# A 2:4-sparse matmul on one core: a new order for the first transposes and their copies, with five tiles of x loaded one by one

## The chip, the cores and the metric

The kernel runs on one core of a Trainium2 chip. The metric is the device time of one execution in microseconds (us), as the median of several runs. Beside it there is one execution recorded by the profiler, whose trace gives every instruction's start and duration; times inside the kernel are given from the start of that trace's span.

## The reference

```python
B, S, D = 16, 512, 1024
def reference(x, w, b):                    # x [16, 512, 1024], w [1024, 1024], b [1024], bf16
    wg = w.reshape(D // 4, 4, D)           # groups of four rows that follow each other
    mag = jnp.abs(wg)
    order = jnp.argsort(mag, 1)
    thr = jnp.take_along_axis(mag, order[:, 2:3, :], 1)    # second largest of the four
    wp = (wg * (mag >= thr)).reshape(D, D)
    return jnp.einsum("bsd,df->bsf", x, wp) + b
```

Of every four neighbouring rows of w only the two largest in each column survive. The pruned matrix is multiplied by 8192 rows of x, and a bias is added.

## The kernel before, in words

**Tiles.** x has 64 tiles of 128 rows. The contraction of 1024 is eight blocks of 128; the halves of it are called groups g = 0 and 1. A block of g = 0 or 1 comes in two layouts. In the "packed" layout (`w_sb`, `wp`) a partition holds one group of four rows, so the four members m = 0..3 of the group lie side by side and pruning is elementwise. In the "natural" layout (`wp_nat`) the rows lie in their own order, one row per partition; DMAs called `spread` (L139) make it from `wp`.

**The head.** While weights arrive and are pruned, TensorE has only what is ready. Tiles 0 to 7 (called NPK) are multiplied with the packed weights of g = 0, as soon as each piece of `wp` exists. Each needs x with the contraction on the partitions, so TensorE transposes the tile in four steps of 128x128 against an identity (`transpose`, L184; four matmuls at L189 into one PSUM buffer `tp`), and ScalarE copies the result to SBUF (`copy_xt`, L192, the copy at L194). The pool `psum_t` (L58) has two buffers, so a transpose waits for the copy of the transpose two before it. `mm_piece` (L205, matmuls at L216) multiplies a transposed tile with one piece of `wp`; a piece is 256 columns of g = 0. Two tiles share one PSUM bank of the pool `psum_o` (L59, six banks), by the list `pairs` (L201): (5, 6), (0, 1), (2, 3), (4, 7). When both tiles of a pair are done with a piece, ScalarE copies the bank to a staging tile (`stage`, L252, the copy at L256), and the bank comes free.

**Who sets the order.** The order on each engine in this head is written out by hand in `order` (L258), as a string of tokens per engine, and kept by program-order dependencies. On TensorE, `T7a` is the transpose of tile 7, `M7.0u` the matmul of tile 7 with piece 0, member 0 (u, v, s, t are members 0 to 3; x and y are pairs of members), `A0h0` the first half of a natural-layout output, `F8` eight dummy matmuls that keep the engine busy before data arrives. On ScalarE, `C7a` is the copy of tile 7's transpose and `S0b0` the staging copy of pair 0 (tiles 5 and 6), piece 0. On VectorE, `abs`, `hi`, `lo`, `t1`, `t2`, `thr`, `mask` and `mult` are the pruning steps; `mult0u` writes member 0 of piece 0 of `wp`. For the change these parts of the strings count:

```python
"pe":  "F8 T7a T5a T6a M7.0u M5.0u M7.0v M5.0v T1a M6.0u M6.0v T0a M7.0s M5.0s M6.0s M7.0t M5.0t M6.0t
        M1.0u M1.0v M1.0s M1.0t M0.0u M0.0v T4a M0.0s M0.0t T3a T2a M4.0u ... M2.0t M4.1x M5.1x M0.1x ..."
"act": "C7a C5a C6a C1a C0a C4a S0b0 C3a C2a S3b0 S1b0 S2b0 abs3 S3b1 ..."
```

**The first loads** are issued by two engines' queues, SyncE's (SP) and ScalarE's (ACT), in the order of L110 to L124. `load_w(g, c0, c1, ma, mb)` loads columns c0 to c1 of members ma to mb of the packed weights, `load_x(ta, tb)` the g = 0 half of tiles ta to tb-1 in one DMA. SP issues, in this order: member 0 and member 2 of weight piece 0 (64 KB each), tiles 5 and 6 in one DMA (256 KB), weight piece 1 (256 KB; "the second weights"), tile 4 (128 KB), tiles 2 and 3 (256 KB), pieces 2 and 3 (512 KB), half of g = 1 (512 KB), the bias, the other half of g = 1. ACT issues members 1 and 3 of piece 0, tile 7 (128 KB) and tiles 0 and 1 in one DMA (256 KB); then comes an activation on a dummy element (`spark`, L116) that brings in the activation table.

**Semaphores of the DMAs.** The framework gives the DMAs eight semaphores in turn. The ninth DMA, and each one after it, is issued only when the DMA eight before it has landed.

**The body and the tail.** After the head, tiles 8 to 63 go through natural-layout matmuls (`nat`, L239): x comes transposed by DMA, two banks per tile, VectorE adds the bias and writes bf16 (L400, L402), ScalarE's queue stores each tile in one DMA of 256 KB. The last `LATE` = 5 tiles are stored in halves (L457), the last tile in four parts.

Of the kernel before, what the change touches and what calls it, by code (L numbers as in the profile page):

```python
# [10 lines left out]
def kernel(  # L11
# [28 lines left out]
    NPK = 8  # L40
    LEAD = 4
    GROUPS = ((0, 5), (5, 8))
    LATE = 5
    sizes = (4, 8, 8, 8, 8, 8, 8)
    batches = []
    t0 = NPK + LEAD
# [29 lines left out]
    def act(i):  # L76
        return seq("act", i)
# [13 lines left out]
    def tokens(dram, t):  # L91
        a, b_ = next(s for s in GROUPS if s[0] <= t < s[1])
        return dram[a * P:b_ * P].rearrange("(p t) k -> p t k", p=P), t - a
    bias_sb = const.tile([P, Dout], bf16)

    def issue(eng, out_, in_):
        q = nc.sync if eng == "sp" else nc.scalar
        return seq(eng, q.dma_start(out_, in_))  # L98

    def load_w(g, c0, c1, ma=0, mb=4, eng="sp"):  # L100
        issue(eng, w_sb[:, g, ma:mb, c0:c1], wv[:, g, ma:mb, c0:c1])

    def load_x(ta, tb, eng="sp"):
        xs = const.tile([P, tb - ta, HK], bf16, name=f"x_{ta}")
        xv, n = tokens(xf, ta)
        issue(eng, xs[:], xv[:, n:n + tb - ta, :HK])
        for t in range(ta, tb):
            x_sb[t] = xs[:, t - ta, :]
# [3 lines left out]
    load_w(0, 0, 256, 2, 3)  # L112
    load_w(0, 0, 256, 3, 4, "act")
    load_x(7, 8, "act")
    load_x(0, 2, "act")
    act(nc.scalar.activation(spark[:], nc.const_aps.tensor(1.0, [P, 1], bf16), Act.Abs))  # L116
    load_x(5, 7)
    load_w(0, 256, 512)
    load_x(4, 5)
    load_x(2, 4)  # L120
    load_w(0, 512, 1024)
# [130 lines left out]
    def stage(q, n):  # L252
        if (q, n // 2) not in staged:
# [3 lines left out]

    order = {  # L258
        "pe": (
            "F8 T7a T5a T6a M7.0u M5.0u M7.0v M5.0v T1a M6.0u M6.0v T0a M7.0s M5.0s M6.0s M7.0t M5.0t M6.0t "  # L260
            "M1.0u M1.0v M1.0s M1.0t M0.0u M0.0v T4a M0.0s M0.0t T3a T2a M4.0u M4.0v M4.0s M4.0t "
            "M3.0u M3.0v M3.0s M3.0t M2.0u M2.0v M2.0s M2.0t M4.1x M5.1x M0.1x M7.1y M6.1y M2.1y M1.1y "
            "M3.1y M6.1x M4.1y M1.1x M3.1x M0.1y M7.1x M2.1x M5.1y M0.2 M3.2 M7.2 M1.2 M2.2 M4.2 "
            "M6.2 M0.3 M2.3 M5.3 M4.3 M5.2 M6.3 M3.3 M1.3 A0h0 A2h0 M7.3 A2h1 A1h0 A3h1 A0h1 A3h0 "
# [6 lines left out]
            "thr5 mask5 mult5"  # L271
        ),
        "act": (
            "C7a C5a C6a C1a C0a C4a S0b0 C3a C2a S3b0 S1b0 S2b0 abs3 S3b1 S1b1 S0b1 S2b1 S2b2 S1b2 "
            "S3b2 S0b2 S1b3 S2b3 W1.0q S3b3 S0b3"
        ),
        "sp": (
# [120 lines left out]
    def evac(o, ps, c0, c1, add=None):  # L398
        if add is None:
            dve(nc.vector.tensor_tensor(o[:, c0:c1], ps, bias_sb[:, c0:c1], op=Alu.add))  # L400
        else:
            dve(nc.vector.tensor_tensor(o[:, c0:c1].rearrange("p (n c) -> p n c", n=2),  # L402
                                        ps.rearrange("p (n c) -> p n c", n=2), add, op=Alu.add))
# [7 lines left out]
    def store(eng, t, o, c0=0, c1=Dout):  # L411
        issue(eng, rows(t)[:, c0:c1], o[:, c0:c1])
# [24 lines left out]
    for bi, (tb, nb) in enumerate(batches):  # L437
        if bi:
            load_batch(bi + 1)
        for j in range(nb):  # L440
# [9 lines left out]
            else:  # L450
# [4 lines left out]
                for h in range(2):  # L455
                    evac(o, pss[h][:], h * FH, (h + 1) * FH)
                    if t >= NT - LATE:  # L457
                        store("act", t, o, h * FH, (h + 1) * FH)
                if t < NT - LATE:
                    store("act", t, o)  # L460
# [30 lines left out]
```

## Time and profile before

| | |
|---|---|
| median of 3 runs | 233.41 us (233.27 to 234.06) |
| the profiled execution's own time | 233.83 us |
| span of its trace, first to last instruction | 232.0 us |
| TensorE (PE) busy | 228.0 us, 98% of the span, 1158 matmuls |
| VectorE (DVE) busy | 107.9 us, 46% |
| ScalarE (ACT) busy | 13.4 us, 6% |
| granted TensorE clock | full speed in all 40 slices |
| last store landed (store issue at 229.75 us, 1.5 us to landing) | 231.2 us |

The span leaves out 1.8 us of the profiled execution's own time that lies around the trace. A row of the timeline gives the start, the length, the engine, the line, the operation, the tiles, the shape and the number of instructions; in brackets stands how long the engine was idle before it and what ended that. "PEld" is TensorE's load of the stationary operand, which runs beside the matmuls. In the chain of waits each row is a step on the path that ended last. A matmul's shown length is longer than the step to the next one, because matmuls are pipelined: four transposes advance TensorE by 0.22 us though one of them is shown with 0.22 us by itself, and twelve matmuls of 256 columns advance it by 1.31 us though one is shown with 0.27 us.

### The profile page before, as it was taken

The numbers are of one execution on the slowest core, as the hardware profiler recorded it, in microseconds if no ns is written. First come the engines' busy times: TensorE is split into PE (matmuls) and PEld (weight loads), VectorE is DVE, ScalarE is ACT, GpSimd is POOL, SyncE is SP. The second block draws the span as 40 slices with busy tenths as digits, with TensorE's granted clock in tenths as the row PEclk, the third lists the DMA queues.
The fourth block names the chain that finished last, engine by engine and source line by source line (L and its number), as shares of the span: only waits on it lengthen the run. The fifth ranks groups of instructions, "written<-read, shape, count | busy, mean of one in ns | idle before, by whom it ended". The sixth has DMA issues, their size and how long they took to land.

```text
span 232.0 us, 2851 instructions
## 1 busy us (share of the span) xinstructions
PE 228.0 (98%) x1158; PEld 112.7 (49%) x1158; DVE 107.9 (46%) x188; ACT 13.4 (6%) x27; POOL 17.6 (8%) x15
## 2 busy tenths in 40 slices
PE   8999999999999999999999999999999999999995
PEld 4887444544444444444444444444444444444443
DVE  4999767754234334334334324424424424423434
ACT  2665100000000000000000000000000000000000
POOL 1000199700000000000000000000000000000000
PEclk9999999999999999999999999999999999999999
DMA  6999999997299321992249821697229942122122
GB/s 192 354 220 211 220 213 227 300 241 272 94 198 275 114 93 51 234 275 76 90 99 250 239 93 47 169 230 198 84 90 191 242 155 76 63 90 81 60 88 90
DMA packets 78268, 38.19 MB, mean 165 GB/s; under 512 B 63664, under 2 KB 70576, under 8 KB 78256
## 3 DMA queue, kind: packets, MB, share of 16 engines
q1 hardware_dynamic: 67328, 20.61, 43.7%
q10 hardware_dynamic: 10928, 17.40, 21.1%
q8 instruction: 9, 0.15, 0.3%
q14 instruction: 3, 0.02, 0.0%
HBM read 3.41 MB, written 16.78 MB: 87 GB/s over the span
## 4 chain that ended last, share of the span: by engine, by line
PE 96%; DMA 2%; ACTq 0%; ACT 0%; DVE 0%; issue 0%
PE ps L239 88%; PE ps L216 6%; DMA x<-in_x_dram 2%; PE tp L239 1%; PE tp L189 1%; ACTq L98 0%; ACT xt L194 0%; DVE o L400 0%
## 5 line engine op out<-in xcount | busy, mean ns | idle before, releaser
L239 PE MATMUL ps<-wp_nat,xb 128*128 128x512 bf16 (+2 forms) x848 | 179.8, 375 | 0.0
L239 PEld LDWEIGHTS <-xb 128*128 128x128 bf16 x848 | 82.4, 98 | 97.5
L400 DVE TENSOR_TENSOR o<-ps,bias_sb 128x512 bf16<-128x512 f32 (+1 forms) x112 | 71.5, 677 | 114.6 <-PE ps L239 114.5
L396 POOL TENSOR_TENSOR st<-st,bias_sb 128x1024 f32<-128x1024 f32 x8 | 16.8, 2131 | 0.0
L216 PE MATMUL ps<-wp,xt 128*128 128x256 bf16 x128 | 15.1, 273 | 0.0
L239 PE MATMUL ps<-wp_nat,xlow 128*128 128x512 bf16 x64 | 14.1, 379 | 0.0
L216 PEld LDWEIGHTS <-xt 128*128 128x128 bf16 x128 | 12.2, 98 | 1.8 <-ACT xt L194 0.2
L402 DVE TENSOR_TENSOR o<-ps,st 128x512 bf16<-128x512 f32 x16 | 11.1, 691 | 2.8 <-PE ps L239 2.3
L239 PE MATMUL ps<-wp_nat,xlead 128*128 128x512 bf16 x48 | 11.2, 379 | 0.0
L239 PEld LDWEIGHTS <-xlow 128*128 128x128 bf16 x64 | 7.2, 112 | 6.7
L239 PEld LDWEIGHTS <-xlead 128*128 128x128 bf16 x64 | 6.3, 98 | 7.1
L256 ACT COPY st<-ps 128x512 f32<-128x512 f32 x16 | 8.5, 598 | 6.3 <-PE ps L216 4.3
L154 DVE TENSOR_TENSOR mag<-mag,hi 128x256 bf16<-128x256 bf16 (+3 forms) x10 | 5.6, 582 | 0.2
L154 DVE TENSOR_TENSOR wp<-w_sb,mag 128x256 bf16<-128x256 bf16 (+3 forms) x10 | 5.6, 580 | 0.1
L133 PE MATMUL ps<-const-bfloat16-1.0 128*128 128x128 bf16 (+1 forms) x22 | 4.3, 394 | 0.8 <-PEq L475 0.8
L164 DVE TENSOR_SCALAR mag<-w_sb 128x512 uint16<-128x512 uint16 (+2 forms) x6 | 2.7, 464 | 3.3 <-DMA w_sb<-in_w_dram 3.3
L239 PE MATMUL tp<-wp_nat,xlead 128*128 128x512 bf16 x16 | 4.1, 379 | 0.0
L133 PEld LDWEIGHTS <-const-bfloat16-1.0 128*128 128x128 bf16 x22 | 2.5, 147 | 2.4 <-issue 2.4
L189 PE MATMUL tp<-ident,x 128*128 128x128 bf16 x32 | 2.9, 219 | 0.6 <-DMA x<-in_x_dram 0.4
L154 DVE TENSOR_TENSOR hi<-mag 128x512 bf16<-128x512 bf16 (+2 forms) x7 | 3.2, 459 | 0.1
L154 DVE TENSOR_TENSOR lo<-mag 128x512 bf16<-128x512 bf16 (+2 forms) x7 | 3.2, 456 | 0.0
L194 ACT COPY xt<-tp 128x256 f32<-128x256 f32 x8 | 2.8, 381 | 3.5 <-PE tp L189 3.5
(15 smaller groups left out, 13.4 us busy)
## 6 DMA issues: line engine op xcount, KB each, us to landing
out_dram<-o ACTq DMA_DIRECT2D x59, 256.0 KB, 2.4
wp_nat<-wp SPq DMA_DIRECT2D x14, 128.0 KB, 3.5
w_sb<-in_w_dram SPq DMA_DIRECT2D x3, 512.0 KB, 6.4
out_dram<-o ACTq DMA_DIRECT2D x8, 128.0 KB, 1.7
x<-in_x_dram SPq DMA_DIRECT2D x2, 256.0 KB, 4.0
w_sb<-in_w_dram SPq DMA_DIRECT2D x1, 256.0 KB, 5.0
x<-in_x_dram ACTq DMA_DIRECT2D x1, 256.0 KB, 4.1
bias_sb<-in_b_dram SPq DMA_DIRECT2D x1, 256.0 KB, 6.4
```

The source lines that it names most:

```text
L133: pe(nc.tensor.matmul(warm_ps[:, :rep * P], lhsT=nc.const_aps.tensor(1.0, [P, P], bf16), rhs=nc.const_aps.tensor(1.0, [P, rep * P], bf16), ...
L154: dve(nc.vector.tensor_tensor(out, a, b_, op=op))
L164: dve(nc.vector.tensor_single_scalar(self.mag[:, ms, :].bitcast(u16), self.w[:, ms, :].bitcast(u16), 0x7FFF, op=Alu.bitwise_and))
L189: pe(nc.tensor.transpose(tp[:, m, :], xg[:, m, :], ident[:]))
L194: act(nc.scalar.copy(xt[:].bitcast(fp32), xpk[t].bitcast(fp32)))
L216: pe(nc.tensor.matmul(ps[:, c0 + d:c1 + d], lhsT=xpk[t][:, m, :], rhs=wp[:, g, m, c0:c1], start=(new and m == ms.start), stop=(left[(q, n) ...
L239: pe(nc.tensor.matmul(ps, lhsT=xt[:, kt - koff, :], rhs=wp_nat[:, kt, c0:c1], start=(kt == first), stop=(kt == last)))
L256: act(nc.scalar.copy(st[:, n % 2, :, :].rearrange("p t c -> p (t c)"), ps_open.pop((q, n))[:]))
L396: pool(nc.gpsimd.tensor_tensor(st[:], st[:], bias[:, :, None, :].to_broadcast([P, 2, 2, CW]), op=Alu.add))
L400: dve(nc.vector.tensor_tensor(o[:, c0:c1], ps, bias_sb[:, c0:c1], op=Alu.add))
L402: dve(nc.vector.tensor_tensor(o[:, c0:c1].rearrange("p (n c) -> p n c", n=2), ps.rearrange("p (n c) -> p n c", n=2), add, op=Alu.add))
```

## The change

Three things are changed. The loads of tiles 5, 6 and of 0, 1 are cut into single tiles: ScalarE's queue loads 7, 6 and 1, SyncE's queue loads 5 ahead of the second weights and 0 behind them. On TensorE the transposes of tiles 1, 4, 3 and 2 stand earlier and apart from each other, and the rest of piece 0 fills in between. On ScalarE the copies of tiles 3 and 2 come ahead of the staging copies, of which pair 3's is now first. Besides, `LATE` goes from 5 to 7, so that two more tiles near the end are stored in halves.

```diff
-    LATE = 5
+    LATE = 7
...
     load_x(7, 8, "act")
-    load_x(0, 2, "act")
+    load_x(6, 7, "act")
+    load_x(1, 2, "act")
     act(nc.scalar.activation(spark[:], nc.const_aps.tensor(1.0, [P, 1], bf16), Act.Abs))
-    load_x(5, 7)
+    load_x(5, 6)
     load_w(0, 256, 512)
+    load_x(0, 1)
     load_x(4, 5)
     load_x(2, 4)
...
         "pe": (
-            "F8 T7a T5a T6a M7.0u M5.0u M7.0v M5.0v T1a M6.0u M6.0v T0a M7.0s M5.0s M6.0s M7.0t M5.0t M6.0t "
-            "M1.0u M1.0v M1.0s M1.0t M0.0u M0.0v T4a M0.0s M0.0t T3a T2a M4.0u M4.0v M4.0s M4.0t "
+            "F8 T7a T5a T6a M7.0u M5.0u T1a M7.0v M5.0v M6.0u M6.0v T0a M7.0s M5.0s M6.0s M7.0t M5.0t M6.0t "
+            "T4a M1.0u M1.0v M1.0s M1.0t T3a M0.0u M0.0v M0.0s M0.0t T2a M4.0u M4.0v M4.0s M4.0t "
...
         "act": (
-            "C7a C5a C6a C1a C0a C4a S0b0 C3a C2a S3b0 S1b0 S2b0 abs3 S3b1 S1b1 S0b1 S2b1 S2b2 S1b2 "
+            "C7a C5a C6a C1a C0a C4a C3a C2a S3b0 S0b0 S1b0 S2b0 abs3 S3b1 S1b1 S0b1 S2b1 S2b2 S1b2 "
```

In the built program the semaphores of the DMAs fall out as follows, for the loads that come after the first eight. Tile 1's load on ScalarE's queue waits for member 1 of weight piece 0, tile 0's for member 0, tile 4's for member 3, the load of tiles 2 and 3 for member 2. The 512 KB of pieces 2 and 3 wait for tile 7, the first half of g = 1 for tile 5, the bias for tile 6, the second half of g = 1 for the second weights. Before, the same four waited for members 3 and 2, for tile 7 and for tiles 5 and 6.

## The prediction

> **What bounds the kernel now.** I read the chain of waits first, because TensorE is busy for 98% of the span and only the chain tells where the rest is.
>
> ```profile
> 1.66 3.79 DMA x<-in_x_dram
> ...
> 5.50 0.43 PE tp L189 x4
> 5.93 0.02 issue
> 5.95 0.38 ACT xt L194
> 6.34 0.04 issue
> 6.38 0.38 PE tp L189 x4
> ...
> 7.86 1.31 PE ps L216 x12
> ...
> 9.62 0.22 PE tp L189 x4
> 9.84 0.02 issue
> 9.86 0.38 PE tp L189 x4
> 10.24 11.47 PE ps L216 x104
> ```
>
> The chain starts with tile 7's load (landed 1.66 + 3.79 = 5.46), goes through its transposes and its copy, and then stays on TensorE until 229.4. So the end moves only by what is saved or lost on TensorE before it runs without gaps. The costs of one step: four transposes advance the engine by 0.22, a matmul of 256 columns by 1.31 / 12 = 0.109.
>
> How much idle is in there? T6 (tile 6's transposes) starts at 6.38, and the timeline shows the first L239 matmul at 21.55: 15.17 us. Between lie T6, T1, T0, T4, T3, T2 (24 transposes, 24 x 0.0555 = 1.33) and 124 of the 128 L216 matmuls (124 x 0.1092 = 13.54), together 14.87. So **0.30 us** of stalls lie behind 6.38. The timeline tells where:
>
> ```profile
> 5.50 0.64 PE L189 MATMUL tp<-ident,x 128*128 128x128 bf16 x8 [0.38 <-DMA x<-in_x_dram]
> ...
> 5.99 0.48 DVE L154 TENSOR_TENSOR wp<-w_sb,mag 128x256 bf16<-128x256 bf16 x2
> ...
> 6.60 0.60 PE L216 MATMUL ps<-wp,xt 128*128 128x256 bf16 x4
> ...
> 9.43 0.37 ACT L194 COPY xt<-tp 128x256 f32<-128x256 f32 x1 [1.16 <-PE tp L189]
> 9.45 0.79 PE L189 MATMUL tp<-ident,x 128*128 128x128 bf16 x8
> 9.70 0.59 ACT L256 COPY st<-ps 128x512 f32<-128x512 f32 x1
> ...
> 10.18 0.67 ACT L194 COPY xt<-tp 128x256 f32<-128x256 f32 x2
> 10.62 5.46 PEld L216 LDWEIGHTS <-xt 128*128 128x128 bf16 x51 [0.23 <-ACT xt L194]
> ```
>
> At 9.45 T3 and T2 stand side by side and take 0.79 where eight transposes need 2 x 0.22 plus 0.16 for the last one's end, 0.61: T2 waits 0.18 for the copy of tile 4 (9.43 to 9.80), whose buffer it takes. At 10.62 the matmuls of tile 3 wait about 0.11 for its copy, which began only at 10.18, because the staging copy S0b0 (9.70, 0.59) stood ahead of it. These two are the 0.30. Ahead of them are two more: T7 waited for tile 7 (last dummy matmul shown to 5.12, T7 at 5.50), and T6 waits for tile 7's copy (C7).
>
> **The order (TensorE and ScalarE).** No instruction is added to either engine's arithmetic. I walk the new order from T6 at 6.38, with the steps above and 0.38 per copy. M7.0u 6.60, M5.0u 6.71, T1 6.82 (its buffer is free at 6.60, the end of row 5.95 0.65), M7.0v and M5.0v 7.04, M6.0u 7.26 (C6 runs 6.80 to 7.18), T0 7.48, six matmuls from 7.70, T4 8.35, M1 8.58, T3 9.01 (C0 done 8.3), M0 9.24, T2 9.67 (C4 8.78 to 9.15), M4 9.90, M3 10.33 (C3 done 9.8), M2 10.77 (C2 done 10.5), M4.1x **11.21**; the same steps with the stalls give 11.51 before. No copy ends last any more. Gain: 0.30.
>
> S0b0 moves behind C3, C2 and S3b0. S3b0 starts when M4.0t ends (10.5); by the row of staging copies "10.72 1.60 x3" one follows the other after (1.60 - 0.6) / 2 = 0.5, so S0b0 ends at 11.6 instead of 10.29. Pair 2's next bank needs it, at M2.1y, eleventh matmul after 11.21: 12.3. Cover 0.7; the bank that S3b0 frees is needed at M0.1x, 11.65, against 11.1. abs3 moves from 12.19 to about 12.5 and ends at 13.6; VectorE's hi3 takes it at 13.84. Cost of all this: nothing; without the cover of 0.2, hi3 moves by as much, and mult3 (done 16.8) has over 1 us until M0.3.
>
> **Tile 7 and the start.** VectorE caps what an earlier tile 7 can bring: M7.0u needs mult0u, which ends at 5.99 + 0.28 = 6.27, and VectorE runs without gaps from 3.27, on weights whose loads stay. With 0.06 for the release, M7.0u starts at 6.33 at best instead of 6.60. So this term lies between 0 and **0.27**, and below 0 only if tile 7 lands later than 5.46. What stands beside it in the queues:
>
> ```profile
> 2.00:3.00 1.00, 1.00 (x4) 0.44 (x3) 0.00 (x0) 0.36 (x1) 0.00 (x0) 1.00 1.05 275
> 3.00:4.00 1.00, 1.00 (x9) 0.72 (x8) 0.70 (x3) 0.99 (x2) 0.00 (x0) 1.00 0.80 249
> 4.00:5.00 1.00, 1.00 (x12) 0.93 (x9) 0.96 (x6) 0.14 (x1) 0.00 (x0) 1.00 1.06 343
> 5.00:6.00 1.00, 0.62 (x10) 0.50 (x9) 0.93 (x6) 0.05 (x1) 0.00 (x0) 1.00 1.00 314
> 6.00:7.00 1.00, 0.76 (x11) 0.62 (x9) 1.00 (x6) 0.81 (x3) 0.00 (x0) 1.00 1.07 364
> ```
>
> The last two columns are the share of the DMA engines and GB/s: they are full from 2 us on. So a load lands by the bytes ahead of it. From the DMA issues, counting 64 KB as 65.5 thousand bytes: up to the end of the second weights both queues together bring 1180 thousand bytes (piece 0 262, tile 7 131, tiles 0 and 1 262, tiles 5 and 6 262, the second weights 262). The rates sum to 1181 at 6.0, and the load lands at 2.11 + 5.0 = 7.1. Tile 4 (1311) lands at 7.5, tiles 2 and 3 (1573) at 8.2: in each case 1.1 us after the rates reach the bytes. Tile 7 landed last of the two loads that were issued at 1.65: tiles 5 and 6, 262 thousand bytes, landed at 1.65 + 3.5 = 5.15. Now only tile 5 goes beside it, 131 thousand bytes less, 0.4 us at 343 GB/s. If all of it went to tile 7 it would land near 5.1 and T7 would start before 5.23, which gives the whole 0.27; if the second weights fill the place at once, nothing. I take 0.2: the transfer that left is larger than the cap.
>
> The Trainium skill's page "DMA: Bandwidth & Descriptors", section "Issuing engines are not separate DMA queues", says that DMAs of the scalar, sync and gpsimd engines run on the same 16 DMA engines and interleave regardless of who started them. That speaks against this part: moving tile 6 to ScalarE's queue would bring tile 7 nothing, and the sum would be 0.30 alone. Here tiles 5 and 6 landed 0.3 us ahead of tile 7 though issued at the same time with twice the bytes, so the queues did not share evenly; the row decides for some gain.
>
> **The other tiles.** Tile 5 is wanted 0.22 after T7 and has less ahead of it than before. Tile 6 is second in ScalarE's queue, tile 1 third; tiles 0 and 1 as second and last in it landed at 2.15 + 4.1 = 6.25, with as many bytes; T1 wants tile 1 at 6.82, or 6.55 with the full gain. Tile 0 stands where the 1180 thousand bytes end: 7.1, and T0 wants it at 7.48, or 7.21. Tiles 4 and 2, 3 keep their bytes (7.5 and 8.2) and are wanted 8.35 and 9.01, or 0.27 sooner. All hold, tile 0 by only 0.1 with the full gain.
>
> Issues: ScalarE's third x load waits for member 1 (landed 3.24) and takes 0.46, so the table load (1.28) and spark (0.20) end near 5.2 instead of 4.1; C7 comes at 5.4 at the earliest. SyncE issues one load more, 0.4 us, in a queue that is ahead of its bytes. The 512 KB of pieces 2 and 3 now wait for tile 7, so they are issued near 5.4 instead of 4.13, and behind them in SyncE's queue the g = 1 weights, the bias and the spreads. The rates reach the bytes ahead of them at 7.1; from issue to landing the 64 KB loads took 2.2 to 2.5 us in all, so their bytes begin before that. Cost: nothing, or up to 0.6 if they begin as late after issue as the second weights' 256 KB did at most (7.7). VectorE wants piece 2 at 10.53, it landed at 9.7: that covers it.
>
> **The tail.** Two more tiles in halves are two more stores of 0.34 us issue in tiles of 3.45 us; the last store is issued at 229.75 behind VectorE's last add (229.43 + 0.29). Nothing of it moves: 0.
>
> **Sum.** 0.30 + 0.2 = 0.5 on the profiled execution: 233.83 - 0.5 = 233.3. That execution is 0.42 above the median of 233.41. If its extra lies in tile 7's wait, the other runs can gain only the 0.30 (233.1); if it lies outside, 233.41 - 0.5 = 232.9. I take the middle, **233.0**.
>
> **Rivals.**
> 1. The order's gain alone (tile 7 lands no sooner, or tile 0 takes back what tile 7 brought): 0.0 to 0.3 less than before, 233.1 to 233.4. For it: the evenly shared engines. Against: 131 thousand bytes fewer in front.
> 2. **Tile 0 comes late, slower.** T0 stands ahead of M7.0s and all that follows, so TensorE waits for it. At landing time L the change loses L + 0.05 - 7.48 - 0.30: slower than before from L = 7.73. The byte count says 7.1; the next load's place says 7.5, the one after 8.2. At 8.2: +0.5, 233.9; over 0.3% only from L = 8.4.
> 3. More than 0.3% (0.70 us, about what a measurement of this kernel can tell from no change) faster. My sum ends at 0.57. It needs runs in which tile 7 landed later than in this trace, which the slowest run (234.06) allows; then 232.4 to 232.7.
> 4. Pieces 2 and 3 late by more than the 0.83 of cover, through their new wait: M0.2 (15.0) has another 1.1 over mult2 (13.9). It only eats the gain: 233.2.
>
> **Numbers.** Forecast (0.3 to 0.57 less) 0.52; rival 1 0.18; rival 2 0.10, of which 0.06 beyond 0.3%; rival 3 0.16; rival 4 0.04. Faster than 0.3% is rival 3 and 0.04 of the forecast for the scatter of the runs (233.27 to 234.06), 0.20; slower 0.06; the rest within. The range takes in rivals 1 and 4, most of 3 and the milder half of 2: 232.4 to 233.8.
>
> **What would show it.** Right: T7 before 5.3; M7.0u at 6.33 to 6.4; T3 and T2 as rows of 0.39 apart from each other; no wait of TensorE for a copy after 7; M4.1x 0.3 to 0.57 before 11.51. Wrong: a wait of L189 for a DMA at T1 or T0, a copy that follows the table load, VectorE idle before piece 2, or a first L239 matmul later than 21.3.

## The result

| | before | change |
|---|---|---|
| median of 19 runs | 233.65 us (233.25 to 234.51) | 234.48 us (234.0 to 235.35) |
| median span of the traces | 231.8 to 232.0 us | 232.3 us |
| own time less span | 1.79 us | 2.15 us |
| last landing of a store to the end of the span | 0.83 us | 1.09 us |

The spans of the kernel before are the medians of its 137 runs beside the experiments, call by call. The ratio is 1.0035, 95% interval 1.0028 to 1.0043: 0.83 us slower, just over the 0.3% that a measurement can tell, where 0.4 us faster was forecast (233.0, range 232.4 to 233.8).

The profiled execution of the change is the fastest of its 19 runs (234.00 us, span 231.8). Its chain of waits (start, length, step) therefore shows what the change does when the loads come in time, to within 0.1 us:

```profile
0.77 4.42 PE ps L135 x22
5.20 0.43 PE tp L191 x4
...
5.65 0.38 ACT xt L196
...
6.07 0.39 PE tp L191 x4
...
9.63 0.22 PE tp L191 x4
9.85 11.35 PE ps L218 x104
```

No load stands in the chain any more. Before, tile 7's load was its first step; now the dummy matmuls are, and the 104 matmuls of the last row end at 21.20 instead of 21.71. The timeline of TensorE in the same profile shows what became of the two waits for copies:

```profile
4.99 0.84 PE L191 MATMUL tp<-ident,x 128*128 128x128 bf16 x8
6.07 0.39 PE L191 MATMUL tp<-ident,x 128*128 128x128 bf16 x4 [0.24 <-ACT xt L196]
6.29 0.38 PE L218 MATMUL ps<-wp,xt 128*128 128x256 bf16 x2
...
8.80 0.39 PE L191 MATMUL tp<-ident,x 128*128 128x128 bf16 x4
...
9.46 0.39 PE L191 MATMUL tp<-ident,x 128*128 128x128 bf16 x4
```

T7 starts at 4.99 instead of 5.50, M7.0u at 6.29 instead of 6.60. T3 (8.80) and T2 (9.46) are rows of 0.39 apart from each other. The last VectorE add starts at 228.92 instead of 229.43, 0.51 earlier. So in this one execution the forecast's 0.5 us is there up to the last add. Yet its span is only 0.2 shorter than the span of the profiled execution before (232.0), its own time is 0.17 us longer, and its fellows are slower still. Three things have to be found: what is lost behind the last add, what is lost outside the span, and what happens in the other executions.

A second profile of the same kernel (run a2 below; span 232.6, own time 234.75) is nearer to the median. Its timeline of TensorE:

```profile
4.88 0.64 PE L191 MATMUL tp<-ident,x 128*128 128x128 bf16 x8 [0.42 <-DMA x<-in_x_dram]
...
6.08 0.38 PE L218 MATMUL ps<-wp,xt 128*128 128x256 bf16 x2
7.04 0.42 PE L191 MATMUL tp<-ident,x 128*128 128x128 bf16 x4 [0.58 <-DMA x<-in_x_dram]
```

The row at 7.04 is T1: TensorE is idle for 0.58 us because tile 1 is not there (it landed at 7.00). That is the row "a wait of L189 for a DMA at T1 or T0" (L189 is L191 in the changed kernel) that the prediction named as what would make it wrong. Its chain of waits:

```profile
1.66 3.17 DMA x<-in_x_dram
4.85 6.84 DMA w_sb<-in_w_dram
11.71 0.44 DVE mag L166
...
14.43 0.70 DVE wp L156
15.18 6.72 PE ps L218 x60
```

Here a second loss follows the first: pieces 2 and 3 of the weights are issued at 4.85, when tile 7 has landed, land at 11.7, and VectorE, after 1.35 us of idle time, passes the delay on to M0.2.

### The profile page after: what moved, and what is told of

It reads as the page before. It is cut to its first block, busy times and chain, and to the rows that moved or that the text cites. A ratio compares the mean times of both kernels' runs of the same rounds, so it can differ in the third digit from the quotient of the medians.

```text
span 231.8 us, 2857 instructions
## 1 busy us (share of the span) xinstructions
PE 227.9 (98%) x1158; PEld 112.8 (49%) x1158; DVE 108.1 (47%) x188; ACT 13.7 (6%) x27; POOL 17.6 (8%) x15
## 4 chain that ended last, share of the span: by engine, by line
PE 98%; ACT 0%; DVE 0%; issue 0%
PE ps L241 88%; PE ps L218 6%; PE ps L135 2%; PE tp L241 1%; PE tp L191 1%; ACT xt L196 0%; DVE o L402 0%
## 5 line engine op out<-in xcount | busy, mean ns | idle before, releaser
L191 PE MATMUL tp<-ident,x 128*128 128x128 bf16 x32 | 3.2, 232 | 0.2 <-ACT xt L196 0.2
```

The source lines that it names most:

```text
L191: pe(nc.tensor.transpose(tp[:, m, :], xg[:, m, :], ident[:]))
```

## The experiments

After the result there were three places for the loss: the head, from loads that come later; the end, from the two tiles more that are stored in halves; and the time outside the traced span. In the texts below, theory A is that the head gains and the loss lies at the end and outside the span ("frame"); theory B is that the loads of the head come late; theory C is that the stores in halves themselves cost. Each experiment has a label. Behind its time stands its ratio to the runs of the kernel before that were made beside it, with the 95% interval in brackets. Two labels with the unchanged kernel before (c0, c1) show how far two labels can differ by nothing.

> The kernel before, unchanged, as a control: ratio 1.000 to within 0.1%. What is wanted of it is the span of every run. Theory A (end and frame: the new kernel's head gains 0.5 us, and the loss lies behind the last store and outside the span): spans of 231.6 to 232.0, so that the new kernel's median span of 232.3 hides a gain of the head, and about 1.8 us outside the span, against 2.2 of the new kernel. Theory B (head: in most runs the single tiles land late, and the profiled run of the new kernel was a lucky one): 2.1 to 2.2 us outside here too, spans near 231.5.

> The kernel before once more, unchanged, to be compared with the others of the same call: the first control came out 0.3 us above the runs of before beside it, by its spans. If every kernel of a call carries such an offset, it is +0.3 again, and the others must be read against this one; if it was chance, 0.0. Outside the span 1.79 us again.

c0 measured 234.03 us, 1.0014 [1.0005, 1.0023]; c1 233.79, 0.9998 [0.9988, 1.0008]. So differences under some 0.15% between labels say nothing by themselves; below they are read only together with a row of a profile.

**e2: only LATE 7.**

```diff
-    LATE = 5
+    LATE = 7
```

> The kernel before with the tail's change alone, two more tiles stored in halves. Theory A: two DMAs more move the last store from the eighth semaphore to the second, so SyncE still has six waits of 0.06 us behind the one that ends last: +0.4 us, and if the time outside the span goes with the number of DMAs or their place, up to +0.3 more; +0.4 to +0.7 in all. Theory B: 0.0. Theory C (the stores in halves themselves cost, by the DMA engines): +0.8, all that was lost and what the head gained in part.

234.27 us, 1.0023 [1.0012, 1.0035]; last landing to end 1.00 us instead of 0.83, outside the span 1.94 instead of 1.79. The prediction had put this edit at 0. Of the 0.63 us over the kernel before these two are 0.32; the rest is no more than c0's 0.39. The expectation counted six waits behind the one that ends last; the trace has three (see e4 and l9).

**e3: only the new orders,** loads and LATE as before.

```diff
-            "F8 T7a T5a T6a M7.0u M5.0u M7.0v M5.0v T1a M6.0u ...
+            "F8 T7a T5a T6a M7.0u M5.0u T1a M7.0v M5.0v M6.0u ...
...
-            "C7a C5a C6a C1a C0a C4a S0b0 C3a C2a S3b0 S1b0 ...
+            "C7a C5a C6a C1a C0a C4a C3a C2a S3b0 S0b0 S1b0 ...
```

> The kernel before with the new orders on TensorE and ScalarE alone, loads and tail as before. Theory A: -0.3 us, all 0.30 of the stalls, and nothing at the end, since the number of DMAs is unchanged. Theory B: -0.3 too. Theory D (the new order of the staging copies or transposes costs something that the profiled run does not show): 0.0 or above.

233.70 us, 1.0005 [0.9995, 1.0015]: no gain in the median against the kernel before. Against c0, the control of the same call, it is 0.33 us less, which would be the whole forecast; as c0 itself is off by 0.39, the medians neither show 0.30 nor shut it out. Its profile has no wait for a copy after 7 us, but tile 7 and tiles 5, 6 landed late in it (T7 at 5.53, M5.0u 0.26 late). So the stalls go; by the profile, other waits at the start are of the same size.

**e4, l9: more tiles in halves.** In every trace SyncE ends the program with five waits, one after the other. Each names two semaphores, and together they take in the eight of the DMAs: the fourth is in the first wait, the second in the second, the eighth in the fifth and last. Which semaphore carries the last store depends on the number of DMAs. e4 has eight DMAs more than the kernel before (four more than the change), so its last store is on the same semaphore as there; l9 is the kernel before with four DMAs more, as many as the change.

e4 is the change with LATE 11, l9 the kernel before with LATE 9:

```diff
-    LATE = 7
+    LATE = 11
...
-    LATE = 5
+    LATE = 9
```

> The changed kernel with four more tiles stored in halves (the last eleven instead of seven), so that the last store falls on the eighth semaphore again, as before the change. Theory A: the four waits behind the last landing go, 0.25 us less than the changed kernel at the end of the span. Theory B: as the changed kernel, +0.8 against before. Theory C: worse than the changed kernel, by 0.2 or more for four more tiles in halves.

> The kernel before with the last nine tiles in halves: four DMAs more than before, as many as the changed kernel has, and the last store on the fourth semaphore as there. If the end goes with the place of the last semaphore: 1.09 us from the last landing to the end (+0.26) and 2.15 us outside the span (+0.35), +0.6 against the control. If the time outside goes with the number of DMAs instead, the same here, but then the kernel with eight more should have had twice that, and it had +0.10. If it belongs to the head's loads: 1.8 to 1.9 outside.

e4: 234.09 us, 1.0017 [1.0006, 1.0028], last landing to end 0.83, outside 1.89. l9: 234.15 us, 1.0016 [1.0004, 1.0028], last landing to end 1.09, outside 1.87. The waits of SyncE (line waited for: us in total, times, longest) for the stores at the end, in before, the change, l9 and e4:

```profile
SPq L486 <- DMA out_dram<-o: 1.4, 4, 0.4
```

```profile
SPq L488 <- DMA out_dram<-o: 1.6, 1, 1.6
```

```profile
SPq L486 <- DMA out_dram<-o: 1.6, 1, 1.6
```

```profile
SPq L488 <- DMA out_dram<-o: 1.4, 4, 0.4
```

Before and in e4 the last stores are waited for one after the other, and the last of all sits on the eighth semaphore: when it lands, no wait is left. In the change and in l9 one wait of 1.6 us takes it all, because the last store sits on the fourth semaphore; the four waits behind it are already satisfied, but each takes about (1.09 - 0.83) / 4 = 0.065 us. e2, with two DMAs more than before, has its last store on the second semaphore, so three waits stand behind it: (1.00 - 0.83) / 3 = 0.06 us each. This is **the end: 0.26 us**, set by the count of DMAs alone; e4 stores more tiles in halves and does not pay it.

**h: the change's head without its tail.** With LATE = 3 the change has as many DMAs as the kernel before.

```diff
-    LATE = 7
+    LATE = 3
```

> The change's head as it is, with the last three tiles in halves instead of seven, so that the number of DMAs is that of the kernel before and the last store falls on the eighth semaphore. Theory A (end and frame): 1.79 us outside the span, 0.83 from the last landing to the end, and the head's gain shows: -0.5 against the control. Theory B (tile 1's load, which is issued only after a weight load has landed, arrives near 7.0 in most runs, and T1 waits): the frame goes as in A, but the spans are those of the control, 0.0 to +0.2; T1 waits for a DMA in the profiled run by 0.4 to 0.6 us.

234.04 us, 1.0014 [1.0005, 1.0024]; outside 1.80, last landing to end 0.83. Both other terms are gone, and the head that was to bring 0.5 us is 0.35 us (0.1 to 0.6) behind the kernel before. c0 was that far off too, so the number alone shows only that the gain is not there; where it goes is in its timeline of TensorE:

```profile
6.31 0.49 PE L218 MATMUL ps<-wp,xt 128*128 128x256 bf16 x2
7.68 0.41 PE L191 MATMUL tp<-ident,x 128*128 128x128 bf16 x4 [0.88 <-DMA x<-in_x_dram]
```

T1 is again what waits: 0.88 us idle, tile 1 landed at 7.63.

**a2: the change once more**, on another chip, beside p1, r1 and v1.

> The changed kernel once more, on the chip and in the call of the others, for its time outside the span and another profile of its head. In the first measurement it was 2.15 us outside, where the kernel before with as many DMAs had 1.87. If that belongs to the program, 2.15 again; if to the chip or the call, 1.85 to 1.9. In the profile T1 waits for a DMA by 0.3 to 1.0 us (theory B), by 0 to 0.1 if the first profile was typical. Time: +0.5 to +0.8 against before.

234.72 us, 1.0043 [1.0029, 1.0056]; outside 2.14. The loss comes again; its profile was read above.

**p1: the change's loads with the old orders. r1: tiles 1 and 6 swapped in ScalarE's queue.** Is it the new order that asks for tile 1 too soon, or the place of the load?

Both are the change with LATE 3; p1 has the orders of e3's removed lines, r1 this:

```diff
-    load_x(6, 7, "act")
     load_x(1, 2, "act")
+    load_x(6, 7, "act")
```

> The change's loads alone, with the orders of before, the last three tiles in halves so that the number of DMAs is that of before. Theory B (tiles 1 and 0 land late, near 7.2): T1 waits 0.2 to 0.8 us, the two old stalls of 0.30 stay or hide in that wait: spans 0.2 to 0.5 above those of before. If the loads are harmless and the orders are what costs: 0.0 to -0.27.

> The kernel with the change's head and as many DMAs as before, tiles 6 and 1 changed about in ScalarE's queue: tile 6 is now the load that waits for a weight load before it is issued. It is wanted at 6.1, tile 1 at 6.5. Theory B: tile 6 lands near 7.2 instead, T6 waits about 1.1 us, and the spans are 0.4 to 0.6 above those with tile 1 in that place, 0.7 to 0.9 above those of before. If the order of the loads does not matter: as with tile 1 there, +0.3.

p1: 234.14 us, 1.0022 [1.0011, 1.0033]. Tile 1 landed at 7.39 and T1 waited 0.61 us in the old order too:

```profile
7.44 0.41 PE L191 MATMUL tp<-ident,x 128*128 128x128 bf16 x4 [0.61 <-DMA x<-in_x_dram]
```

r1: 236.14 us, 1.0077 [1.0047, 1.0107]. Now tile 6 is the ninth DMA: it landed at 7.35, and TensorE stood idle for 1.70 us before T6 (the row is in the last section). So it is the place, whichever tile has it. Two of r1's six runs took 234.4 and 234.6, 0.7 and 0.9 us above the kernel before, as expected; the other four are slower for a further reason, which the last section gives. The ninth DMA waits for member 1's landing and is issued near 3.0 instead of some 2.6, behind the second weights (issued at 2.11) and tile 0 (2.84 in h). The issues of tiles 1 and 0 (us from issue to landing) in h, where both are issued between 2.84 and 3.02, on two queues:

```profile
x<-in_x_dram SPq DMA_DIRECT2D x1, 128.0 KB, 5.0
x<-in_x_dram ACTq DMA_DIRECT2D x1, 128.0 KB, 4.6
```

They land at 7.8 and 7.6, side by side, though tile 1 is third in ScalarE's short queue and tile 0 stands behind 512 KB on SyncE's. In this profile the place in the queue does not count; the bytes issued before by both queues do. That holds only roughly: in p1 and in the fastest run of the change tile 1 landed 0.45 and 0.74 us ahead of tile 0, though it was issued 0.2 us behind it.

**g1: tile 6 beside tile 5 again, so that tile 1 is the seventh DMA. v1: tile 1 the eighth, and tiles 1 and 0 ahead of the second weights.** Both start from the change, g1's diff first:

```diff
-    LATE = 7
+    LATE = 4
-    load_x(6, 7, "act")
-    load_x(5, 6)
+    load_x(5, 7)
```

```diff
-    LATE = 7
+    LATE = 3
-    load_x(1, 2, "act")
+    x1 = load_x(1, 2, "act")
...
+    load_x(0, 1, after=x1)
     load_w(0, 256, 512)
-    load_x(0, 1)
```

> The change's orders, with tiles 5 and 6 in one DMA on SyncE as before and tile 1 second on ScalarE's queue, so that its load is the seventh DMA and waits for nothing; the last four tiles in halves, so that the number of DMAs is that of the kernel before. Theory B: T1 no longer waits (tile 1 lands by 5.5), M4.1x comes 4.6 to 4.7 us after M7.0u, and the time is 0.3 to 0.5 below the control and below the kernel with the change's head. Theory A: the same as that kernel, -0.5.

> The change's orders and single tiles, but tile 1's load takes the eighth semaphore, so that it is issued at once, and tile 0's goes ahead of the second weights, which wait in turn; as many DMAs as before. Theory B: tile 1 lands by 5.6, tile 0 by 6.7, tile 7 by 5.0, no wait of TensorE for a DMA after T7; the second weights land near 7.2 and VectorE, which wants them at 7.05, waits 0.1 to 0.3 with 0.8 us to spare; spans 0.4 to 0.6 below those of before, near 231.4, and 0.7 below those with the change's head. If something else in the new head costs: at or above before.

g1: 233.81 us, 0.9999 [0.9988, 1.0010]; tile 1 issued at 2.15, landed at 5.43. Its timeline of TensorE has no wait for a load behind M7.0u:

```profile
6.35 0.38 PE L217 MATMUL ps<-wp,xt 128*128 128x256 bf16 x2
6.57 0.39 PE L190 MATMUL tp<-ident,x 128*128 128x128 bf16 x4
...
7.23 0.39 PE L190 MATMUL tp<-ident,x 128*128 128x128 bf16 x4
```

One load joined again, and the waits of the head are gone, with the new orders in place. Its profiled execution is 0.5 us shorter in span than that of before (231.5 against 232.0), as forecast for the change; its median is not, and the interval (-0.3 to +0.2 us) does not reach a gain of 0.5 us. The profiled execution is the second fastest of its eleven. v1: 234.45 us, 1.0033 [1.0022, 1.0045]: a miss. Tiles 1 and 0 came in time, but the timeline shows the wait one step later, at T4:

```profile
7.17 0.39 PE L194 MATMUL tp<-ident,x 128*128 128x128 bf16 x4
...
8.88 0.41 PE L194 MATMUL tp<-ident,x 128*128 128x128 bf16 x4 [0.66 <-DMA x<-in_x_dram]
```

The windows by stage (from:to, length, busy us of PE, PEld, DVE, ACT, POOL, granted clock, share of the DMA engines, GB/s) say why; from 2 to 11 us in before and the change, and from 6 to 8 us in v1:

```profile
2.00:11.00 9.00, 8.36 (x80) 6.66 (x79) 7.46 (x29) 4.83 (x12) 0.00 (x0) 1.00 1.02 326
```

```profile
2.00:11.00 9.00, 8.76 (x85) 7.24 (x84) 7.53 (x28) 5.06 (x12) 0.00 (x0) 1.00 0.97 294
```

```profile
6.00:8.00 2.00, 1.93 (x24) 1.70 (x23) 1.72 (x8) 1.42 (x5) 0.00 (x0) 1.00 0.66 198
```

The stream of loads has gaps: 294 GB/s instead of 326 in the change, 198 in v1 where before has 358 from 6 to 8 us. The five profiles with the change's head (its two, e4, h and t1) have 293 to 303, the five with the head of before (before, c0, c1, e2 and l9) 319 to 331. Each load past the eighth is issued when the one eight before it lands. Smaller loads then leave fewer bytes under way; that this is what makes the gaps is argued, no run tests it apart. v1, where another order was to mend it, only handed the delay on to tile 4.

**w2, w3: fewer loads ahead.** If the turn of the semaphores is the cause, two DMAs less for the first weights must bring tile 1's issue forward with the change's loads (w2); w3 joins the new orders, the old x loads and the shorter start. w2 has LATE 5, w3 LATE 7; both have this:

```diff
-    load_w(0, 0, 256, 0, 1)
-    load_w(0, 0, 256, 1, 2, "act")
-    load_w(0, 0, 256, 2, 3)
-    load_w(0, 0, 256, 3, 4, "act")
+    load_w(0, 0, 256, 0, 2)
+    load_w(0, 0, 256, 2, 4, "act")
```

> The change's orders and single tiles, with weight piece 0 in two loads of two members instead of four, so that tile 1 and tile 0 are the seventh and eighth DMA and are issued at once, tile 4 and tiles 2, 3 after the first weights; as many DMAs as before. Theory of the DMAs in flight: tile 1 lands by 5.6, tile 0 near 6.9, tile 4 by 7.6; no wait of TensorE for a DMA after T7 above 0.1; VectorE starts up to 0.2 later than now; spans 231.3 to 231.7, 0.3 to 0.5 below those of before. If small loads are late as such: T1, T0 or T4 waits again, and the spans are at 232.0 or above.

> The change's orders with the loads of before (tiles 5, 6 and 0, 1 in pairs) and weight piece 0 in two loads, the last seven tiles in halves; as many DMAs as before. No load of x waits for another before it is issued. Theory of the DMAs in flight: as the orders alone, or better by the earlier issue: spans 231.4 to 231.8, 0.1 to 0.5 below before, with T7 (5.0 to 5.6) as what scatters.

w2: 233.95 us, 1.0012 [1.0003, 1.0022], with a median span of 232.1 where 231.3 to 231.7 was expected; tile 1 issued at 2.27, landed at 6.71 and not by 5.6, T1 at most 0.1 late. From issue to landing that is 4.4 us, as in h (4.6): only the issue came sooner. The head's wait is gone, but VectorE starts on the first weights at 3.43 instead of 3.0 to 3.3, since two members now come in one load. w3: 233.59 us, 1.0002 [0.9994, 1.0011]. Its profiled execution is its slowest (234.22 us), and it speaks against the turn of the semaphores as the only cause: tiles 0 and 1 waited for nothing before their issue at 1.78, yet landed at 7.44, and T1 waited 0.66 us. Tile 4 and tiles 2, 3 were issued earlier there as well (at 2.46 and 3.11), so more loads were under way by then; that this is what delayed tiles 0 and 1 is not shown. No version here is measurably faster than the kernel before.

**k5, k8, t1: the time outside the span.** It is 1.79 in before and 1.78 to 1.81 in h, e3, g1, p1, r1, v1, w2 and w3, but 2.15 in the change, 1.94 in e2, 1.87 in l9 and 1.89 in e4. More stores on ScalarE's queue, or a longer program? k5 and k8 add nothing but dummy activations of one element each on ScalarE, behind its spark; t1 keeps the change's stores and gives the first halves of the six late tiles to SyncE.

k5's diff to the kernel before (8 in k8), and t1's to the change:

```diff
+    for _ in range(5):
+        act(nc.scalar.activation(spark[:], nc.const_aps.tensor(1.0, [P, 1], bf16), Act.Abs))
...
-                        store("act", t, o, h * FH, (h + 1) * FH)
+                        store("act" if h else "sp", t, o, h * FH, (h + 1) * FH)
```

> The kernel before with five more dummy activations of one column on ScalarE, where it waits for tile 7 anyway; DMAs and orders unchanged. If the length of ScalarE's program sets the time outside the span (183 recorded instructions there, as in the changed kernel, instead of 178): 2.1 us outside. If it goes with the DMAs or their semaphores: 1.79.

> The same with eight more (186 instructions on ScalarE, as the kernel before with nine tiles in halves, which had 1.87 us outside). By the length of the program: 1.85 to 1.9. By the DMAs: 1.79. The three more may delay tile 7's copy by 0.1 to 0.3 us inside the span.

> The changed kernel with the first halves of the six tiles near the end issued by SyncE instead of ScalarE: the same 138 DMAs or so on the same semaphores, the last on the fourth, but twelve recorded instructions fewer on ScalarE (171). Theory of the program's length: 1.79 to 1.80 us outside the span instead of 2.14, the rest unchanged: 1.09 from the last landing to the end, less what SyncE has waited for already, and spans near 232.4; +0.4 to +0.6 against before. If the time outside goes with the change's loads or DMAs: 2.14 again, +0.8.

k5: 233.87 us, 1.0009 [0.9999, 1.0019], outside **2.13**, with no DMA added and a span as before (231.75 against 231.8). k8: 234.12 us, 1.0017 [1.0003, 1.0031], outside 1.87 or 1.88 in three of its four runs and 2.43 in the fourth (the profiled one). Both came out as expected from the length of ScalarE's program: kernels whose traces have the same number of instructions on ScalarE have the same time outside, whatever their DMAs. With 183 instructions it is 2.15 in the change and 2.13 in k5, with 186 it is 1.87 in l9 and in three runs of k8. t1: 234.70 us, 1.0033 [1.0009, 1.0057], outside 2.04 where 1.79 to 1.80 was expected: ScalarE's program is shorter than before's (171 instructions against 178), but SyncE's is longer (73 against 60). So the length of an engine's program moves this time, not the stores as such. That is **outside the span: 0.36 us** in the change. By which rule stays open: it does not rise evenly (1.80 with 181 instructions in w3, 1.94 with 182 in e2, 1.89 with 191 in e4), and t1 speaks against ScalarE's length alone.

## Why the prediction was wrong

**The order, 0.30: right in its mechanism.** Both waits for copies are gone in the change's, e3's and g1's profiles. In g1 M4.1x starts 4.61 us after M7.0u, the length that the walk gave; in the five profiles with the head of before (before, c0, c1, e2 and l9) it starts 4.91 to 5.02 after. The median of e3 leaves the gain open; in its profile tiles 7, 5 and 6 came late instead.

**Tile 7, 0.2: right for the one profile that it was read from, too much for the others.** T7 starts at 4.99 and 4.88, M7.0u at 6.29 and 6.08 in the change's two profiles, instead of 6.60. That is past the cap of 6.33, because VectorE began on the weights sooner as well (3.09 and 3.02 instead of 3.27; c0, c1, e2 and l9 have 2.95 to 3.07, so this is not the change's doing). But the profile that the prediction read had tile 7 late: it landed at 5.46, where the middle one of the five profiles with the head of before has 5.11, and in three of these (c0, e2, l9) tile 7 landed ahead of tiles 5 and 6 and not last. With the change's head the middle one of five lands at 4.68, so the load does come 0.4 us sooner, as the bytes said. M7.0u is only 0.04 us sooner (6.31 against 6.35 in the middle profiles): in four of the five T7 follows the dummy matmuls, which are shown to 5.20, without any wait for tile 7.

**The other tiles: this is the step that failed first.** "Tile 6 is second in ScalarE's queue, tile 1 third; tiles 0 and 1 as second and last in it landed at 2.15 + 4.1 = 6.25, with as many bytes". Tile 1 landed at 6.45 in the fastest run, and at 7.00 to 7.63 in five further profiles of these loads (a2, e4, h, t1, p1). The text counted bytes in order of issue for tile 0, over both queues (7.1, measured 7.2 to 7.8; that the engines are full from 2 us on is not quite so, its row from 3 to 4 us has a share of 0.80), but for tile 1 it took over the landing of a load that was issued at 2.15. Tile 1's issue waits for member 1, at 3.0, and tile 0's at 2.84 already stands ahead: by the text's own byte rule it is tile 1 that ends at 1180 thousand bytes, 7.1. T1 wanted it at 6.55 to 6.82, so this was a loss of 0.3 to 0.55 by the prediction's own numbers; T1 came 0.4 to 1.05 us late in a2, e4, h and t1 (TensorE idle for 0.24 to 0.88). Rival 2 had the mechanism, but for tile 0. With tile 1's 6.82 in place of 7.48 its working gives a change that is slower from a landing at 7.07 on, and five of the six profiles have 7.00 to 7.63.

The Trainium skill's page "DMA: Bandwidth & Descriptors", section "Issuing engines are not separate DMA queues", says that the loads of both queues interleave on the same engines; h's two landings agree (7.6 and 7.8). The prediction weighed it against tile 7 alone and not for tile 1, where it mattered more.

**Pieces 2 and 3: a size.** Their new wait was put at nothing, or up to 0.6 within the cover of 0.83. They landed at 9.69 before, at 10.56 in the fastest run of the change, and at 10.5 to 11.8 in the other profiles of these loads. In a2 VectorE waited for them, as its timeline shows:

```profile
11.71 0.43 DVE L166 TENSOR_SCALAR mag<-w_sb 128x1024 uint16<-128x1024 uint16 x1 [1.35 <-DMA w_sb<-in_w_dram]
```

and M0.2 came 0.22 us late: from M4.1x to M0.2 it is 3.71 us in a2, and 3.49 to 3.50 in the other four profiles with the change's head and in the five with the head of before. So the cover held but for a2, though VectorE was idle for 0.38 us in e4 and 0.48 in h. Rival 4 came to pass in a2, beside the late tile, not instead of it.

**The tail, 0: failed.** No store waits longer, but the count of DMAs moved the last store from the eighth semaphore to the fourth, which costs 0.26 us at the end (l9 has it, e4 and h don't).

**Outside the span:** the prediction took the 1.8 us around the trace as a constant. It is 0.36 us more.

The sum: 0.36 outside, 0.26 at the end, and what is left of 0.83 us, 0.21, in the head. That is in place of a gain of 0.5; h alone measures the head at 0.35 (0.1 to 0.6), which agrees within what the control c0 allows. The traces say the same: the last VectorE add starts at 229.57 in the middle one of the five profiles with the change's head and at 229.38 in the middle one of the five with the head of before, 0.19 later (the first five reach from 228.92 to 230.01, the others from 228.96 to 229.92). In the head it is T1 that turns the gain into a loss: M7.0u to M4.1x takes 4.71 us in the fastest run, and 5.06 to 5.78 in the other four. By size the two terms that the prediction put at nothing, the end and the time outside, are 0.62 of the 0.83. One thing stays open: the gain that the profiles of the change and of g1 show behind M7.0u is not seen in g1's median and left open by e3's, though nothing that these profiles show takes it back.

## What to carry to other kernels

Cutting a load in two spends a turn of the DMA semaphores: look up which landing each later load must wait for, when that lets it be issued, and count the bytes that all queues have issued by then, for every tile by the same rule. (The rule is rough: it gave 7.1 for tile 1, and six profiles have 6.45 to 7.63.) Let the load that is needed last be the one that stands last in order of issue. When the number of DMAs or instructions changes, compare the last landing to the end and the own time less the span too, and don't judge by one profile: the one shown may be the fastest run, and the one a gain is read from may have an unusual wait in it.

## What the runs showed of the hardware

r1's late tile 6 cost more than its wait. Its timeline of TensorE and its windows around it:

```profile
5.06 0.64 PE L191 MATMUL tp<-ident,x 128*128 128x128 bf16 x8 [0.44 <-DMA x<-in_x_dram]
7.40 0.61 PE L191 MATMUL tp<-ident,x 128*128 128x128 bf16 x4 [1.70 <-DMA x<-in_x_dram]
```

```profile
7.00:8.00 1.00, 0.60 (x5) 0.56 (x6) 0.97 (x4) 0.00 (x0) 0.00 (x0) 0.60 0.83 258
8.00:9.00 1.00, 1.00 (x9) 0.85 (x7) 0.96 (x4) 0.47 (x2) 0.00 (x0) 0.50 0.89 292
9.00:10.00 1.00, 1.00 (x9) 0.80 (x8) 0.97 (x4) 0.27 (x1) 0.00 (x0) 0.50 0.91 296
10.00:11.00 1.00, 1.00 (x10) 0.78 (x8) 0.53 (x2) 0.37 (x1) 0.00 (x0) 0.69 1.07 298
```

After 1.70 us of idle time, with a gap of 0.44 and eight transposes ahead of it, the granted clock is 0.50 until some 10.6 us (the last row mixes 0.50 and 1.00), and the matmuls take twice as long: four transposes advance TensorE by 0.43 us instead of 0.22. Four of r1's six runs have the lower mean clock of this one (0.993; 236.1 to 236.3 us), the other two, at full clock, took 234.4 and 234.6. T1's 0.58 and 0.88 us of idle time in a2 and h left the clock at full speed. The Trainium skill's page "TensorE: Matmul & The Clock Gate", section "Part 1: The HAM clock gate (the "warmup" mystery)", puts the halving at one idle window or more, about 3.4 us; here 1.70 us at a stretch, 2.14 with the gap before it, were enough.
